# One result block of the last group turned back on VectorE instead of TensorE, and PSUM pairs that alternate across experts

## The chip, the cores and the metric

The kernel runs on one core of a Trainium2 chip. The metric is the device time of one execution in microseconds (us). TensorE (PE, with its weight loads PEld), VectorE (DVE), ScalarE (ACT), GpSimd (POOL) and SyncE (SP) each work through their own instruction queue in program order; they wait for one another through semaphores. Transfers between DRAM and the on-chip memory SBUF are DMAs, most of them issued by SyncE. Matmuls write PSUM, which has eight banks of 128 x 512 fp32.

## The reference

```
# attention, blocks of 64 with a carried state: q, k, v are (4, 8, 768, 64)
out[block] = ((q k^T) * decay mask) v + (q * lam_pow) kv_state
kv_state   = lam_block * kv_state + (k * rev_pow)^T v
# bridge: x is (3072, 512), then four experts, all of them over all tokens
p   = domain_probs / (domain_probs.sum(-1) + 1e-9)
out = sum over e of p[:, e] * (relu(x @ w1[e]) @ w2[e])      # w1 512x1024, w2 1024x512
```

All of it is fp32. The output is 3072 x 512.

## The kernel before

**Groups and units.** The 3072 tokens are three groups of 1024. A *unit* is a group with an expert, so there are twelve, `units[0]` to `units[11]`; `at` is the unit's number. While a unit's second matrix product (h times w2) runs, TensorE also runs the first product (x times w1) of the unit after it (`ahead`), in alternation: the list `order` has eight places, four of the second product `b` and four of the first product `a`. The last unit (`at` 11, group 2, expert 3) has no first product beside it.

**Strassen twice.** Each product is a Strassen-Winograd product of seven block products named M1 to M7, and the first product is split the same way once more: seven outer times seven inner products. In the last group (`nested`) the second product is nested too. `nested_product(e, m, tags)` (from line 1084) gives the steps of one outer product: seven inner products in the order `INNER` = M1, M7, M6, M4, M5, M2, M3, each two fp32 matmuls of 128x256 (the trace has two records for each fp32 matmul). Inner products M1, M6, M5, M3 go to the PSUM bank `tags[0]`, the others to `tags[1]`. M1, M7 and M2 start their bank anew; before M1 does so, whatever was read last from that bank must have been read. After each inner product VectorE adds the bank to a tile `sums[m]` in SBUF (line 1114); for expert 0 some of these are copies on ScalarE (line 1112).

**PSUM pairs.** The outer products of one expert come in the order `SEQ3` = M1, M3, M5, M7, M6, M2, M4 (index `i`). With a unit ahead they take the pairs (q01, q02) and (q11, q12) by `i % 2`, so that products 1 and 7 both have (q01, q02). In the last unit three pairs rotate by `i % 3`, the third being (g1, g3), which the first product uses otherwise.

**The last group is computed turned.** Its second product has features on the partitions and tokens along the rows: `sums[m]` is a tile [128, 4, 256], and `sums[m][:, 2*dd + t]` holds 128 features of block `dd` for 256 tokens of block `t`. After the last expert, the `sums` of M1 to M7 are joined into the four result blocks M2, M3, M4 and M5 (`RESULT`, line 1008). `to_join(m)` fills the list `joins` with steps; each brings one half of a `sums` tile into a PSUM bank with a copy on ScalarE (`bring`, line 968) or adds such a bank to another `sums` tile on VectorE (`add`, line 972). After M6 there are nine steps, and one is taken at each place of the order (`joined()`). In VectorE's queue the product M2's stage then has: M6 into M7 and M3 (three additions), the drain of M2's first bank, M6 into M3's second half, M7 into M4 (two), M7 into M5's first half, the drain of M2's second bank, M7 into M5's second half.

**M2 of the last expert** is a plain product (`plain_product`, line 1032): four parts of eight matmul records, at places 1, 3, 5 and 7 of the order, on banks g1 and g3.

**Turning back.** `give(m, t, tags, dds)` (line 1010) turns a block back: TensorE transposes (128x128, line 1018) into bank s0 or s1, a copy on ScalarE (line 1022) into a tile `y`, and a store by SyncE (line 1024): with both `dds` 256 rows of 1 KB. It first calls `joined(m)`, which takes steps from `joins` until none is left that adds to m. `after_last` says at which places this happens. In the last unit's product M2, M3's two halves are given at places 6 and 7; in its product M4 the halves of M5 and M2 at places 1 to 4. M4's own block is given at the very end: `turn_end`, `turned_product` and two calls of `give` with one `dd`, inserted into `b`.

**Transposes on VectorE in 32x32 blocks** exist already for q and k of some chunks (line 516, `turn_across`), together with copies in DRAM in pieces of 128 bytes (`bring_across`, line 367), issued by SyncE.

Of the kernel before, what the change touches and what calls it, by code (L numbers as in the profile page):

```python
# [22 lines left out]
def kernel(  # L23
# [30 lines left out]
    nc = tc.nc  # L54
# [4 lines left out]
    P = nc.NUM_PARTITIONS  # L59
# [4 lines left out]
    G = CPG * C  # L64
    NG = NTOK // G
    Q = G // 4
    DH = DOUT // 2
    W = 512
# [19 lines left out]
    def bank(tag, name):  # L88
        return ps.tile([P, W], FP32, name=name, tag=tag)

    def small(name):
        return pool.tile([P, W], FP32, name=name, tag="t")
# [329 lines left out]
    for r in range(2):  # L422
        for ac in range(NHP):
            h = 4 * r + ac
            nc.vector.tensor_tensor_scan(
                out=s_decay[:, r, ac], data0=lam_bc[:, h:h + 1].to_broadcast([P, C]), data1=ident[:],
# [9 lines left out]
    m = 1  # L436
    while m < C:
        nc.vector.tensor_tensor(
            out=q_decay[:, :, m:2 * m], in0=q_decay[:, :, 0:m],
# [44 lines left out]
    def take(queue, force=False):  # L484
        for x, f in enumerate(queue):
            if force or getattr(f, "at", 0) <= now[0] and getattr(f, "can", lambda: True)():
                queue.pop(x)()
                return

    def rest(n=1, force=False):  # L490
        for _ in range(n):
            take(background, force)
# [181 lines left out]
    LAST = NG - 1  # L674
# [252 lines left out]
    SEQ3 = ("M1", "M3", "M5", "M7", "M6", "M2", "M4")  # L927
    sums = {}
# [28 lines left out]
    joins, apart, there = [], [], {}  # L957

    def join(a, b):
        def step():  # L960
            x, y = (sums[m][:].rearrange("p k t -> p (k t)") for m in (a, b))
            tt(nc.gpsimd, x, x, y, ALU.add)
            apart.remove(a)

        apart.append(a)
        aside.append(step)
# [8 lines left out]
        x = sums[a][:, 2 * k:2 * k + 2].rearrange("p k t -> p (k t)")  # L975
        tt(nc.vector, x, x, there[b, k][:], ALU.add)

    def joined(m=None):

        while m in apart:  # L980
            take(aside, True)
        while joins and (m is None or any(m in x for x, _ in joins)):
            joins.pop(0)[1]()
            if m is None:
                return

    def to_join(m):

        def steps(*work):
            for fs in work:  # L990
                joins.append(([x[1] for x in fs if x[0] == add], lambda fs=fs: [x[0](*x[1:]) for x in fs]))

        if m == "M3":
            steps(
                [(bring, "M1", 0, "q01")], [(bring, "M1", 1, "q02"), (add, "M6", "M1", 0)], [(add, "M6", "M1", 1)],
            )
        if m == "M5":
            join("M3", "M5")
            join("M2", "M1")
        if m == "M6":  # L1000
            steps(
                [(bring, "M6", 0, "s0")], [(bring, "M6", 1, "s1"), (add, "M7", "M6", 0)], [(add, "M3", "M6", 0)],
                [(bring, "M7", 0, "q11"), (add, "M7", "M6", 1)], [(bring, "M7", 1, "q12"), (add, "M3", "M6", 1)],
                [(add, "M4", "M7", 0)], [(add, "M4", "M7", 1)], [(add, "M5", "M7", 0)], [(add, "M5", "M7", 1)],
            )


    RESULT = {"M2": (0, 0), "M3": (0, 1), "M4": (1, 0), "M5": (1, 1)}

    def give(m, t, tags, dds=(0, 1)):  # L1010

        joined(m)
        i, j = RESULT[m]
        p, o = bank(tags[t % len(tags)], "yp"), small("y")
        w = len(dds) * P
        for x, dd in enumerate(dds):
            for s in range(2):
                nc.tensor.transpose(
                    out=p[:, s * w + x * P:s * w + (x + 1) * P], in_=sums[m][:, 2 * dd + t, s * P:(s + 1) * P],
                    identity=ident[:],  # L1020
                )
        nc.scalar.copy(out=o[:, 0:2 * w], in_=p[:, 0:2 * w])
        r, d = LAST * G + j * W + t * 256, i * DH + dds[0] * P
        nc.sync.dma_start(
            out=out[r:r + 256, d:d + w].rearrange("(s p) d -> p s d", p=P),
            in_=o[:, 0:2 * w].rearrange("p (s d) -> p s d", s=2),
        )


    PLAIN = E - 1, "M2"  # L1030
# [23 lines left out]
    END = E - 1, SEQ3[-1]  # L1054
    ends = []

    def turn_end(t, tag):

        joined(END[1])
        p = bank(tag, "yp")  # L1060
        for s in range(2):
            nc.tensor.matmul(
                out=p[:, s * P:(s + 1) * P], lhsT=sums[END[1]][:, t, s * P:(s + 1) * P], rhs=ident[:],
                is_transpose=True, start=(s == 0), stop=True, skip_group_check=True,
            )
        ends.append(p)
# [300 lines left out]
    def pause_till(i, x):  # L1367
# [13 lines left out]

    fill3 = [(e, m, k) for e in range(E) for m in SEQ3 for k in range(4)]
    after_last = {
        "M2": (None,) * 5 + (("M3", 0), ("M3", 1)),
        "M4": (("M5", 0), ("M5", 1), ("M2", 0), ("M2", 1)),
    }
    steps = attention(1)
    PACE = 1.0, 1.4, 1.0
    for at, (g, e) in enumerate(units):
        if at == 0:  # L1390
            chores.extend(prepare_w2(2) + prepare_w1(3) + prepare_w2(3) + prepare_w1(0))
        ahead = units[at + 1] if at + 1 < len(units) else None
        nested, nests = g == LAST, ahead and ahead[0] == LAST
        if g == LAST - 1:
            if e == 0:
                chores.append(turn_gates)
            chores.extend(prepare_w2_ops(e))
        if ahead and ahead[1] == 0:
            assert not steps
            steps = attention(ahead[0] + 1) if ahead[0] + 1 < NG else []  # L1400
        if at == 3:
            bring_across(3)
        blocks, banks = {}, {}
        for i in range(7):
            if fill2:
                feed2(*fill2.pop(0))
            if nested or (nests and i == 6):
                for _ in range(2 if ahead else 16 if i == 0 else 4 if i > 1 else 0):
                    if fill3:
                        feed3(*fill3.pop(0))  # L1410
            if nests and i == 2:
                nc.scalar.dma_start(
                    out=gate_bc, in_=gate_rows[:, ahead[1]].partition_broadcast(P),
                )
            if nested:
                b = nested_product(e, SEQ3[i], (("q01", "q02"), ("q11", "q12"), ("g1", "g3"))[i % (2 if ahead else 3)])
                if i < 6 and (e, SEQ3[i + 1]) != PLAIN:
                    inner_sums(e, SEQ3[i + 1])
            else:
                b = second_product(g, e, SEQ2[i], banks)  # L1420
            if nests and i == 6:
                inner_sums(ahead[1], SEQ3[0], nested)
                if ahead[1] == EARLY[0]:
                    inner_sums(*EARLY, True)
            a = []
            if ahead:
                a = first_product(*ahead, SEQ[i], blocks, ("g1", "g3"))
            if (e, SEQ3[i]) == END:
                b[6:6] = [lambda: (give("M4", 1, ("s0", "s1"), (1,)), turn_end(1, "q11"))]
                b[5:5] = [lambda: (give("M4", 0, ("s0", "s1"), (1,)), turn_end(0, "q12"))]  # L1430
            if not ahead:
                order = [[], b[0:2], [], b[2:4], [], b[4:6], [], b[6:]]
            elif nested:
                order = [b[0:2], a[0:2], b[2:4], a[2:4], b[4:6], a[4:6], b[6:8], a[6:8]]
            else:
                order = [b[0:1], a[0:2], b[1:2], a[2:4], b[2:3], a[4:6], b[3:5], a[6:8]]
            turned_back = list(after_last.get(SEQ3[i], ())) if nested and not ahead else []
            for x, part in enumerate(order):
                for f in part:
                    if f:  # L1440
                        f()
                now[0] += 1
                if joins:
                    joined()
                elif (ahead or x % 2 == 0 and x + i) and not (nests and i == 6 and x == 7):
                    rest()
                if nested or nests:
                    take(aside)
                if at == 0:
                    take(own_sums)  # L1450
                if nested and ahead and x in (1, 3) and fill3:
                    feed3(*fill3.pop(0))
                if turned_back and x > 0:
                    y = turned_back.pop(0)
                    if y:
                        give(*y[:2], ("s0", "s1"), *y[2:])
                if x == 0 and at * 7 + i >= 6 and fill:
                    feed(*fill.pop(0))
                if at == 0 and x == 0 and i < AHEAD:
                    load(CPG + i)  # L1460
                if steps and (at > 0 or i > 1) and (x == 5 or (x == 2 and i in (1, 3, 5) and at not in (0, 3))):
                    steps.pop(0)()
                if x % 2:
                    trickle()
                pump(PACE[g])
# [30 lines left out]
```

## Time and profile before

| | |
|---|---|
| time of four runs | 1186.0, 1186.87, 1187.85, 1189.48 us; median 1187.36 |
| the profiled execution: its time | 1187.19 us |
| its span, first to last instruction | 1185.4 us |
| granted TensorE clock | 1.00 |
| unit 8 to 9, 9 to 10, 10 to 11 | near 964, 1049 and 1134 us |
| last unit, products M1 to M6 | 1134 to 1165 us |
| last unit, product M2 | 1165 to 1173 us |
| last unit, product M4 and the end | 1173 us to the end |
| last store issued | 1182.54 us |
| DMA traffic | 324 MB, mean 274 GB/s |

The page of a profile gives the busy time of each engine, the span in slices, the chain of work that ended last, and groups of instructions by line and tile. A *timeline* row gives the start in us, the time that the group took, the engine, the line, the operation, output and input tiles, the shape, the count, and in brackets the idle time before it with what ended that idle time. A *waits* row says who waited for whom: total us, times, longest. A row of one line's instructions gives the shortest, median and longest duration in ns. Lines are those of the kernel; line 95 is the helper `tt` through which all tensor-tensor operations pass, so there one goes by the tile's name.

### The profile page before, as it was taken

Reading aid. Unit: us, or ns where it says so; the run is one execution under the profiler, and the core shown is the slowest. Engines: PE = TensorE matmul, PEld = TensorE weight load, DVE = VectorE, ACT = ScalarE, POOL = GpSimd, SP = SyncE. Lnnn points to the kernel's source line nnn. Section 1 sums busy time; section 2 is a strip of 40 time slices with the busy share of each in tenths; the row PEclk is TensorE's granted clock in tenths of the full one; section 3 lists DMA queues with packets and bytes.
Section 4 is the critical chain, followed back from the end, with each engine's and each line's share of the span. In section 5 each row is a group of like instructions: output and inputs, shape, how many; then the busy total and the mean of one; then the engine's idle time right before and its main releaser. Section 6 shows DMA issues by size and latency. Waiting matters only on the chain.

```text
span 1185.4 us, 17886 instructions
## 1 busy us (share of the span) xinstructions
PE 1178.2 (99%) x6567; PEld 1024.3 (86%) x6567; DVE 790.7 (67%) x1329; ACT 275.0 (23%) x502; POOL 628.3 (53%) x600
## 2 busy tenths in 40 slices
PE   9999999999999999999999999999999999999998
PEld 8888888888888888888888888888888888888887
DVE  5785785567478857647756764773665676777784
ACT  3332122112111201211220120121243342341332
POOL 2756258349457800055244655416584683783884
PEclk9999999999999999999999999999999999999999
DMA  9798798999999997899997989898986657566542
GB/s 224 201 279 255 244 304 308 342 339 335 359 366 337 317 297 221 254 284 335 295 298 248 288 291 316 273 307 304 317 294 233 257 189 273 209 239 246 213 160 90
DMA packets 261927, 324.23 MB, mean 274 GB/s; under 512 B 117296, under 2 KB 203216, under 8 KB 261840
## 3 DMA queue, kind: packets, MB, share of 16 engines
q1 hardware_dynamic: 252288, 320.40, 81.3%
q10 hardware_dynamic: 9552, 2.69, 1.2%
q8 instruction: 52, 0.85, 0.3%
q14 instruction: 35, 0.29, 0.1%
HBM read 237.69 MB, written 89.54 MB: 276 GB/s over the span
## 4 chain that ended last, share of the span: by engine, by line
PE 91%; DVE 3%; SPq 2%; DMA 2%; issue 0%; ACT 0%; POOL 0%; ACTq 0%; DVEq 0%
PE pg L843 38%; PE q L897 31%; PE pq L1104 13%; PE pc L1234 2%; PE sp L551 1%; PE op L579 1%; SPq L123 1%; PE pM L1234 1%; DMA w_ops<-ops 1%; DVE hS L95 1%; DVE m L95 1%; DMA w_ops<-w2b 1%; PE op L574 1%; PE op L587 1%; PE pM L1039 1%; SPq L341 0%
## 5 line engine op out<-in xcount | busy, mean ns | idle before, releaser
L843 PE MATMUL pg<-xs_in,ws_in 128*128 128x256 f32 x1960 | 469.8, 380 | 1.1 <-DVE m L95 1.1
L843 PEld LDWEIGHTS pg<-xs_in,ws_in 128*128 128x128 f32 x1960 | 371.3, 190 | 53.1 <-DVE m L95 2.5
L95 DVE TENSOR_TENSOR m<-pg,m 128x512 f32<-128x512 f32 x451 | 307.7, 687 | 106.1 <-PE pg L843 98.8
L897 PE MATMUL q<-w2t,hS 128*128 128x256 f32 x1024 | 243.4, 380 | 0.0
L897 PEld LDWEIGHTS q<-w2t,hS 128*128 128x128 f32 x1024 | 193.2, 190 | 27.0 <-issue 0.2
L913 DVE SCALAR_TENSOR_TENSOR acc<-q,gate,acc 128x256 f32<-128x256 f32 x192 | 92.5, 482 | 169.4 <-PE q L897 169.2
L897 PE MATMUL q<-w2t,m 128*128 128x256 f32 x768 | 182.7, 381 | 0.0
L897 PEld LDWEIGHTS q<-w2t,m 128*128 128x128 f32 x768 | 144.8, 190 | 20.5 <-issue 0.3
L855 ACT ACTIVATE m<-m 128x512 f32<-128x512 f32 x132 | 82.9, 630 | 284.3 <-DVE m L95 283.6
L95 POOL TENSOR_TENSOR m<-m,xT 128x512 f32<-128x512 f32 x64 | 80.6, 1274 | 72.8 <-ACT m L855 55.1
L95 POOL TENSOR_TENSOR kn<-kn,s_decay 128x512 f32<-128x512 f32 x20 | 22.9, 1146 | 142.2 <-PE kp L529 136.4
L95 DVE TENSOR_TENSOR sums<-pq,sums 128x256 f32<-128x256 f32 x153 | 64.3, 421 | 47.4 <-PE pq L1104 40.2
L851 ACT COPY m<-pg 128x512 f32<-128x512 f32 x88 | 51.5, 585 | 174.9 <-PE pg L843 172.1
L1104 PE MATMUL pq<-acc,w2t 128*128 128x256 f32 x352 | 86.6, 379 | 0.0
L95 POOL TENSOR_TENSOR ops<-w2b 128x256 f32<-128x256 f32 x24 | 17.8, 762 | 121.3 <-DMA w2b<-in_moe_w_dram 113.7
L1104 PEld LDWEIGHTS pq<-acc,w2t 128*128 128x128 f32 x352 | 66.8, 190 | 9.3 <-issue 0.3
L95 POOL TENSOR_TENSOR acc<-hT,hT 128x512 f32<-128x512 f32 x32 | 40.2, 1271 | 31.3 <-PE pq L1104 29.4
L95 POOL TENSOR_TENSOR w2o<-w2b 128x512 f32<-128x512 f32 x32 | 40.5, 1288 | 24.8 <-DMA w2b<-in_moe_w_dram 16.4
L786 ACT ACTIVATE m<-m 128x512 f32<-128x512 f32 x44 | 27.7, 631 | 103.1 <-DVE m L95 103.1
L95 DVE TENSOR_TENSOR m<-m,m 128x512 f32<-128x512 f32 x56 | 50.3, 897 | 0.0
L95 DVE TENSOR_TENSOR hS<-m,m 128x512 f32<-128x512 f32 x56 | 46.1, 826 | 4.9 <-ACT m L855 4.9
L95 POOL TENSOR_TENSOR acc<-hT,acc 128x512 f32<-128x512 f32 x32 | 40.7, 1273 | 7.4 <-PE pq L1104 5.4
(157 smaller groups left out, 1360.4 us busy)
## 6 DMA issues: line engine op xcount, KB each, us to landing
xs_in<-x_ops SPq DMA_DIRECT2D x70, 896.0 KB, 6.1
ws_in<-w_ops SPq DMA_DIRECT2D x70, 896.0 KB, 8.7
w2t<-w_ops SPq DMA_DIRECT2D x66, 256.0 KB, 6.6
w2t<-w_sums SPq DMA_DIRECT2D x64, 256.0 KB, 3.9
w_ops<-ops SPq DMA_DIRECT2D x28, 512.0 KB, 5.5
w2t<-in_moe_w_dram SPq DMA_DIRECT2D x48, 256.0 KB, 3.3
w2b<-in_moe_w_dram SPq DMA_DIRECT2D x32, 256.0 KB, 6.1
w_sums<-w2o SPq DMA_DIRECT2D x16, 512.0 KB, 4.9
```

Source lines behind the costliest of these rows:

```text
L95: eng.tensor_tensor(out=o, in0=a, in1=b, op=op)
L123: by.dma_start(out=to[:, :, r], in_=of[:, :, r])
L551: nc.tensor.matmul(out=sp[r][:, ac * C:(ac + 1) * C], lhsT=hc(kT)[half[r], ac], rhs=hc(qT)[half[r], ac], start=True, stop=True,)
L574: nc.tensor.matmul(out=op[r][half[x], a * C:(a + 1) * C], lhsT=kv[half[r], 2 * a + x], rhs=hc(qs)[half[r], 2 * a + x], start=(a == 0), sto ...
L786: nc.scalar.activation(out=o[:], in_=o[:], func=AF.Relu)
L843: nc.tensor.matmul(out=p[:, j * 256:(j + 1) * 256], lhsT=ws[i][:, j * P:(j + 1) * P], rhs=xs[i], start=(fresh and j == 0), stop=True, skip ...
L851: nc.scalar.copy(out=new[at][:], in_=p[:])
L855: nc.scalar.activation(out=new[at][:], in_=new[at][:], func=AF.Relu)
L897: nc.tensor.matmul(out=p[:, s * DH:(s + 1) * DH], lhsT=h[A_OF[m]][:, c * 256 + s * P:c * 256 + (s + 1) * P], rhs=fed2[g, e, m][uu][:, c], ...
L913: nc.vector.scalar_tensor_tensor(out=o, in0=x, scalar=w, in1=o, op0=ALU.mult, op1=ALU.add)
L1104: nc.tensor.matmul(out=p[:, 0:256], lhsT=fed3[e, m, x // 2][:, x % 2, c * P:(c + 1) * P], rhs=b[B_OF[i]][:, c * 256:(c + 1) * 256], start= ...
L1234: nc.tensor.matmul(out=p[:, s * 256:(s + 1) * 256], lhsT=a[c][:, f:f + P], rhs=b[:, c, j * 256:(j + 1) * 256], start=(s == 0 and c == 0 an ...
```

## The change

Three edits.

1. M3's result block no longer goes through `give`. A new function `give_across` lets VectorE transpose each half `sums["M3"][:, 2*dd + t]` (128x256) in 32x32 blocks into a tile `y` and, when both `t` of a `dd` are there, issues four stores, one for each 32 partitions of the tile: 512 pieces of 128 bytes, 64 KB. The second of each four is issued by ScalarE, the others by SyncE. It happens at places 3 (`dd` 0) and 5 (`dd` 1) of product M2, where `give` for M3 stood at 6 and 7.
2. `joined` takes a `k`: with it, only the additions to that half of a block are waited for. `joins` notes pairs (block, half) for that.
3. With a unit ahead, the PSUM pair is chosen by `(at * 7 + i) % 2` instead of `i % 2`. The last unit keeps `i % 3`.

The condition `nested and` before END changes nothing that is emitted: without nesting `b` is shorter than the places where the two calls are inserted, and they are never run.

```diff
-    def joined(m=None):
+    def joined(m=None, k=None):
 
         while m in apart:
             take(aside, True)
-        while joins and (m is None or any(m in x for x, _ in joins)):
+        while joins and (m is None or any(m == x and k in (None, y) for to, _ in joins for x, y in to)):
             joins.pop(0)[1]()
             if m is None:
                 return
...
-                joins.append(([x[1] for x in fs if x[0] == add], lambda fs=fs: [x[0](*x[1:]) for x in fs]))
+                joins.append(([(x[1], x[3]) for x in fs if x[0] == add], lambda fs=fs: [x[0](*x[1:]) for x in fs]))
...
+    halved = {}
+
+    def give_across(m, dd, t):
+
+
+        joined(m, dd)
+        i, j = RESULT[m]
+        if t == 0:
+            halved[m, dd] = small("y")
+        o = halved[m, dd]
+        nc.vector.transpose(out=o[:, t * 256:(t + 1) * 256], in_=sums[m][:, 2 * dd + t])
+        r, d = LAST * G + j * W, i * DH + dd * P
+        for a in range(4 * t):
+            by = nc.scalar if a == 1 else nc.sync
+            by.dma_start(
+                out=out[r:r + W, d + a * 32:d + (a + 1) * 32].rearrange("(b p) d -> p b d", p=32),
+                in_=o[a * 32:(a + 1) * 32].rearrange("p (b d) -> p b d", d=32),
+            )
...
     after_last = {
-        "M2": (None,) * 5 + (("M3", 0), ("M3", 1)),
-        "M4": (("M5", 0), ("M5", 1), ("M2", 0), ("M2", 1)),
+        "M2": ((), (), (("M3", 0, 0), ("M3", 0, 1)), (), (("M3", 1, 0), ("M3", 1, 1))),
+        "M4": ((("M5", 0),), (("M5", 1),), (("M2", 0),), (("M2", 1),)),
     }
...
             if nested:
-                b = nested_product(e, SEQ3[i], (("q01", "q02"), ("q11", "q12"), ("g1", "g3"))[i % (2 if ahead else 3)])
+                pair = (at * 7 + i) % 2 if ahead else i % 3
+                b = nested_product(e, SEQ3[i], (("q01", "q02"), ("q11", "q12"), ("g1", "g3"))[pair])
...
-            if (e, SEQ3[i]) == END:
+            if nested and (e, SEQ3[i]) == END:
...
                 if turned_back and x > 0:
-                    y = turned_back.pop(0)
-                    if y:
-                        give(*y[:2], ("s0", "s1"), *y[2:])
+                    for y in turned_back.pop(0):
+                        if SEQ3[i] == END[1]:
+                            give(*y[:2], ("s0", "s1"), *y[2:])
+                        else:
+                            give_across(*y)
```

## The prediction

> **What bounds the kernel.** I read the page's busy times first, then the waits of TensorE from 950 us on (the change touches nothing earlier), then the timelines around the changes of expert and around the last seventeen microseconds.
>
> ```profile
> PE 1178.2 (99%) x6567; PEld 1024.3 (86%) x6567; DVE 790.7 (67%) x1329; ACT 275.0 (23%) x502; POOL 628.3 (53%) x600
> ```
> ```profile
> PEld pq L1104 <- ACT sums L1112: 0.9, 1, 0.9
> PEld pq L1104 <- ACT m L855: 0.8, 2, 0.4
> ```
>
> TensorE is the clock of this kernel: 7.2 us of the span are not matmul. A microsecond is won only by taking matmuls off TensorE or by closing one of its few gaps. The second fence shows gaps: before the first weights of an expert's first product the weight load waited once 0.9 us, and twice 0.4 us. These are the three changes of expert inside the last group, at 964, 1049 and 1134 us.
>
> **Part 1: alternating PSUM pairs.** Before, product 7 of an expert and product 1 of the next both used q01/q02, so product 1 had to wait until the last block of product 7 had been read out of q01. With (at*7+i)%2 experts 0 to 1 and 1 to 2 change pairs (units 8, 9, 10 begin with pair 0, 1, 0). Unit 10 ends on pair 0 and unit 11 begins on pair 0 (i%3), so the wait at 1134 us stays. It adds no instruction.
>
> ```profile
> 962.82 1.03 PE L843 MATMUL pg<-xs_in,ws_in 128*128 128x256 f32 x4
> 964.35 1.13 PE L1104 MATMUL pq<-m,w2t 128*128 128x256 f32 x4 [0.51 <-ACT sums L1112]
> 965.32 1.03 PE L1104 MATMUL pq<-acc,w2t 128*128 128x256 f32 x4
> 966.18 0.60 PE L843 MATMUL pg<-xs_in,ws_in 128*128 128x256 f32 x2
> ```
>
> Eight of these matmul records take 1.73 us on the chain of waits, 0.216 us each. From 962.82 to 966.18 twelve records stand: 12 x 0.216 = 2.59, but 3.36 passed, so this change of expert costs **0.77 us** (the wait and a slow start of 0.1 to 0.2 us after it). In the same way 1048.20 to 1051.06 is 2.86, a cost of **0.27 us**. There the name ACT m is misleading: the record ahead of the weight load waited until 1049.20, just behind VectorE's read of q01 (1048.74 + 0.41 = 1049.15).
>
> What is late next? After two parts of the second product TensorE returns to the first product and needs bank g1, whose last reader on VectorE is an addition that waits for ScalarE, not for TensorE:
>
> ```profile
> 964.03 0.69 DVE L95 TENSOR_TENSOR hT<-hp,m 128x512 f32<-128x512 f32 x1 [0.59 <-ACT hp L702]
> 964.64 0.68 DVE L95 TENSOR_TENSOR m<-pg,m 128x512 f32<-128x512 f32 x1
> ```
>
> It ends at 965.32. The g1 weight load, at 965.97 before, would come at 965.20 and must wait to about 965.37; the second g1 matmul then starts near 965.69 (0.32 us after such a load, as at 964.35 to 964.67) in place of 966.40. Of 0.77 us 0.71 is left. At 1050 us the same addition ends at 1050.70; its load moves from 1050.84 to 1050.75, the second matmul from 1051.27 to about 1051.07: 0.20 of 0.27 is left. GpSimd's sums are in time (the one for the third part ends at 965.22, needed at 967.1). DMA was busy 0.62 to 0.66 of these stretches, so I cost the earlier loads at nothing; if they were late, the gain would shrink to zero, not below. Sum: **-0.91 us**, between 0 and -1.04.
>
> **Part 2: M3's block turned on VectorE.** It removes from TensorE eight transposes in two lots of four, the x4 rows below, and from ScalarE two copies of 0.585 us and from SyncE two stores.
>
> ```profile
> 1165.43 5.34 PE L1039 MATMUL pM<-m,w2s 128*128 128x256 f32 x24
> 1170.61 0.60 PE L1018 MATMUL yp<-ident,sums 128*128 128x128 f32 x4
> 1171.04 1.89 PE L1039 MATMUL pM<-m,w2s 128*128 128x256 f32 x8
> 1172.77 0.60 PE L1018 MATMUL yp<-ident,sums 128*128 128x128 f32 x4
> 1173.21 1.03 PE L1104 MATMUL pq<-hT,w2s 128*128 128x256 f32 x4
> 1174.08 1.03 PE L1104 MATMUL pq<-acc,w2s 128*128 128x256 f32 x4
> 1174.94 1.04 PE L1018 MATMUL yp<-ident,sums 128*128 128x128 f32 x8
> ```
>
> From 1170.61 to 1171.04 and from 1172.77 to 1173.21 is 0.87 us of TensorE, with no wait. In their place VectorE gets four transposes of 128x256 ahead of work that TensorE needs soon:
>
> ```profile
> L516 DVE STREAM_TRANSPOSE qx<-qx x8: 700/702/703, 335.6 to 650.7; 128x512 f32<-128x512 f32 x8
> ```
> ```profile
> 1169.15 0.69 DVE L95 TENSOR_TENSOR sums<-pM,sums 128x512 f32<-128x512 f32 x1 [0.56 <-PE pM L1039]
> 1169.76 2.47 DVE L95 TENSOR_TENSOR sums<-sums,jp 128x512 f32<-128x512 f32 x4
> 1172.97 0.69 DVE L95 TENSOR_TENSOR sums<-pM,sums 128x512 f32<-128x512 f32 x1 [0.75 <-PE pM L1039]
> 1173.58 0.68 DVE L95 TENSOR_TENSOR sums<-sums,jp 128x512 f32<-128x512 f32 x1
> ```
>
> A 128x512 transpose holds the engine as long as a 128x512 addition (0.62 to the next start against 0.60). 128x256 additions follow one another at 0.34 to 0.35, so I take 0.35 for the half-size transpose; the bounds are 0.31 (half) and 0.62 (no saving). Program order on VectorE becomes: drain, join of M3, two transposes, two joins of M4, two transposes, first join of M5, drain, second join of M5. From 1169.15, which TensorE sets as before: 0.61 + 0.60 + 0.70 + 1.20 + 0.70 + 0.60 + 0.61 + 0.68 = 5.70, so the second join of M5 ends at **1174.85** where it ended at 1174.26.
>
> That join is what M5's turning-back waits for. TensorE, 0.87 us earlier, would load the first weights that depend on it at 1174.18 (1175.05 before). It waits to about 1174.89: 0.71 of the 0.87 us is handed back, and a slow restart takes up to 0.1 more. Left is **-0.1 us**. With 0.31 for a transpose 0.3 is left; with 0.62 the wait is 1.8 us and the change loses 0.9. Behind the waiting transposes stand M4's reads of q01/q02; they come at 1174.8 to 1175.5, before TensorE needs the banks again at 1175.6 and later. ScalarE's two fine stores wait for the transposes until 1171.1 and 1173.0, and its next copy is due only at 1175.4.
>
> One page of the Trainium skill leans the other way, in favour of the edit: "VectorE: DVE Perf Modes", section "The three transpose paths", prices a 128x128 bf16 transpose at 390 ns on TensorE and 311 ns on VectorE. By that as an estimate eight times 390 ns, 3.1 us, would leave TensorE. The rows say 0.11 us for each transpose on TensorE, so the gain cannot reach that.
>
> **The fine stores.** Eight stores of 512 pieces of 128 bytes take the place of two with 256 pieces of 1 KB. The nearest row is the copy of q and k between DRAM buffers, of the same 512 pieces of 128 bytes:
>
> ```profile
> L367 SPq DMA_DIRECT2D across<-in_q_dram x32: 562/680/3231, 66.7 to 446.2; - x32
> ```
>
> Issue takes 0.56 to 3.23 us, median 0.68; the long ones stood in full queues (DMA shares near 1), while here no packet moves between 1168 and 1172 us. Six on SyncE at 0.62 each run from 1171.2 to 1175.0; M5's first store is due at 1176.0, so there is 1 us of slack. A packet of 128 bytes took 13 ns against 46 ns for 1 KB: 4096 x 13 / 16 engines = 3.3 us of DMA against 512 x 46 / 16 = 1.5 us, over by about 1179, with the last store issued at 1182.5. Cost: nothing; if the cover is gone, see the third rival. "DMA: Bandwidth & Descriptors", section "Specifications", speaks against the edit: below 512 bytes a transfer does a read-modify-write. It gives no time for it; per byte the packet rows already show 128 bytes at 2.2 times the cost of 1 KB.
>
> **Sum.** -0.91 - 0.1 = -1.0 us. The profiled execution took 1187.19 us (span 1185.4 and 1.8 around it), the median of the four runs is 1187.36. So 1186.2 for the profiled execution, **1186.4 us** for the median. Not over 0.2% (2.4 us), which is about what a measurement of this kernel can tell from no change; the runs before alone span 1186.0 to 1189.5.
>
> **Rivals.**
> - *Everything is kept* (15%): VectorE keeps up, and all 0.77 + 0.27 + 0.87 = 1.9 us stay: 1185.5. For it: VectorE was idle 0.56 and 0.75 us in this stage. Against: the new transposes need 1.4.
> - *The changes of expert win nothing* (15%): another wait stands right behind (the g1 bank, or the loads) and part 2 also gives back its gain: 1187.3. For it: the g1 bank is within 0.2 us of being that wait at both places.
> - *Slower: SyncE's issue of fine stores delays the last store* (9%). If each of the six takes p, M5's store starts at 1171.2 + 6p and the last one seven stores of 0.49 later. That passes the old 1182.4 once p is over 1.3 us. At 1.93, as one such issue at 403 us took in a busy stretch, the last store starts at 1186.2, 3.8 us late: about 1190.2 with part 1's gain. Against it: idle queues.
> - *The alternation does not do all it says*: unit 10 to 11 keeps its wait. This is already in the sum.
>
> The forecast has the remaining 61%, its own range 1185.7 to 1187.0. Run-to-run spread moves a median by about 0.8 us; with the first rival's 1185.5 and the second's 1187.3 the range is 1184.6 to 1188.4, which leaves out the third and little else. Faster by over 0.2% (below 1185.0) needs the first rival and a lucky median: 13%. Slower by over 0.2% (above 1189.7) is the third rival, with a little for longer transposes plus an unlucky median: 11%. Within: 76%.
>
> **What would show it.** Part 1: no wait on ACT sums before the weight load near 964, none near 1049, still one near 1133; g1's weight load waits for VectorE instead. Part 2: no x4 rows of L1018, four STREAM_TRANSPOSE rows of about 0.43 us between 1169 and 1173, and one new wait of about 0.7 us of M5's transposes for VectorE. Fine stores: issue near 0.6 us, none unfinished when the last store is issued. The prediction is wrong if that issue is over 1.3 us, or if TensorE meets M5 without a wait.

## The result, and the profile after

The changed kernel takes 1186.32 us in the median of 34 runs (1184.63 to 1187.72), the kernel before 1187.82 us in 52 runs (1185.88 to 1191.18). The ratio is 0.9988 with a 95% interval of 0.9983 to 0.9993: about 1.4 us less (0.8 to 2.0 by the interval), clear of no change, but inside the 0.2% that the prediction gave as about the least that can be told from it. The profiled execution has a span of 1184.4 us (1185.4 before).

So small a difference is read from stretches of the trace, not from whole times. The start of the last group's second product moves from run to run by more than the change is worth: its first matmul record stands at 879.08 us before, at 879.48 after, and between 879.05 and 881.20 in the experiments. From that record on, two executions of the changed kernel agree to 0.01 us, record by record; so do the kernels here that use the same PSUM pairs, up to product M2. I call the stretch from it to the last matmul record the *nested part*; it lasts 302.75 us before and 301.54 after.

The waits of the weight loads from 950 us on, after:

```profile
PEld pg L1123 <- DVE sums L95: 0.7, 1, 0.7
PEld yp L1018 <- DVE sums L95: 0.6, 1, 0.6
PEld pg L843 <- DVE m L95: 0.4, 2, 0.2
PEld pq L1123 <- ACT m L855: 0.4, 1, 0.4
```

(Line 1123 is line 1104 of before, 1058 is 1039.) The 0.9 us for ACT sums is gone, one of the two 0.4 us for ACT m is left, and three waits stand where the prediction put them: two of 0.2 us for bank g1 at the changes of expert, one of 0.6 us at the transposes. The 0.7 us of the first row were there before too.

The first change of expert on TensorE, and the weight loads and VectorE's queue at the second:

```profile
963.23 1.03 PE L843 MATMUL pg<-xs_in,ws_in 128*128 128x256 f32 x4
964.09 1.03 PE L1123 MATMUL pq<-m,w2t 128*128 128x256 f32 x4
964.95 1.03 PE L1123 MATMUL pq<-acc,w2t 128*128 128x256 f32 x4
```
```profile
1049.41 0.84 PEld L1123 LDWEIGHTS pq<-acc,w2t 128*128 128x128 f32 x4
1050.45 1.59 PEld L843 LDWEIGHTS pg<-xs_in,ws_in 128*128 128x128 f32 x8 [0.20 <-DVE m L95]
```
```profile
1049.11 0.69 DVE L95 TENSOR_TENSOR hT<-hp,m 128x512 f32<-128x512 f32 x1 [0.25 <-ACT hp L702]
1049.72 0.68 DVE L95 TENSOR_TENSOR m<-pg,m 128x512 f32<-128x512 f32 x1
```

Product 1's matmuls follow without a gap. Two parts later the load for g1 starts at 1050.45, 0.05 us after the addition that reads g1 ends (1049.72 + 0.68). A gap was closed and a shorter one opened behind it.

The stage of product M2 and the start of M4, TensorE and VectorE:

```profile
1172.70 1.03 PE L1123 MATMUL pq<-acc,w2s 128*128 128x256 f32 x4
1173.56 0.38 PE L1018 MATMUL yp<-ident,sums 128*128 128x128 f32 x2
1174.29 0.87 PE L1018 MATMUL yp<-ident,sums 128*128 128x128 f32 x6 [0.35 <-DVE sums L95]
1175.00 1.89 PE L1123 MATMUL pq<-acc,w2s 128*128 128x256 f32 x8
```
```profile
1168.65 0.69 DVE L95 TENSOR_TENSOR sums<-pM,sums 128x512 f32<-128x512 f32 x1 [0.56 <-PE pM L1058]
1169.26 0.68 DVE L95 TENSOR_TENSOR sums<-sums,jp 128x512 f32<-128x512 f32 x1
1169.86 0.76 DVE L1039 STREAM_TRANSPOSE y<-sums 128x256 f32<-128x256 f32 x2
1170.55 1.24 DVE L95 TENSOR_TENSOR sums<-sums,jp 128x512 f32<-128x512 f32 x2
1171.72 0.75 DVE L1039 STREAM_TRANSPOSE y<-sums 128x256 f32<-128x256 f32 x2
1172.39 0.65 DVE L95 TENSOR_TENSOR sums<-sums,jp 128x512 f32<-128x512 f32 x1
1172.97 0.68 DVE L95 TENSOR_TENSOR sums<-pM,sums 128x512 f32<-128x512 f32 x1
1173.57 0.67 DVE L95 TENSOR_TENSOR sums<-sums,jp 128x512 f32<-128x512 f32 x1
```

The eight transposes of M5 (2 + 6) took 0.87 us before; now 1.44 us pass from 1173.56 to 1175.00. TensorE does the two that need only M5's first half, then waits until VectorE's last row above is done (1174.24). VectorE no longer waits for the second drain, as it did before for 0.75 us: it comes late to it.

### The profile page after: what moved, and what is told of

It is laid out like the page before. It is cut to its first block, busy times and chain, and to the rows that moved or that the text cites. A ratio compares the mean times of both kernels' runs of the same rounds, so it can differ in the third digit from the quotient of the medians.

```text
span 1184.4 us, 17880 instructions
## 1 busy us (share of the span) xinstructions
PE 1176.6 (99%) x6559; PEld 1023.0 (86%) x6559; DVE 791.4 (67%) x1333; ACT 274.0 (23%) x500; POOL 629.0 (53%) x600
## 4 chain that ended last, share of the span: by engine, by line
PE 91%; DVE 3%; DMA 3%; SPq 1%; POOL 1%; issue 0%; ACT 0%; ACTq 0%; DVEq 0%; POOLq 0%
PE pg L843 37%; PE q L897 30%; PE pq L1123 13%; PE pM L1253 2%; PE pc L1253 2%; PE op L579 2%; PE sp L551 2%; DMA w_ops<-ops 2%; DMA w_ops<-w2o 1%; PE op L574 1%; DVE hS L95 1%; SPq L123 1%; DVE m L95 1%; PE op L587 1%; DVE sums L95 0%; PE kp L529 0%
```

## The experiments

Theory: TensorE sets the time; the alternation wins 0.71 and 0.20 us, the turning wins its 0.87 us less what VectorE's longer queue makes TensorE wait at M5, and the fine stores cost nothing where they stand. Rivals: the gain lies in stretches that the change does not touch; it lies mostly in the turning; the wait at M5 is for something else; the fine stores cost time.

| kernel | nested part, us | last matmul to the end, us | ratio to before, 95% interval |
|---|---|---|---|
| before | 302.75 | 3.58 | 1 |
| changed | 301.54 | 3.41 | 0.9988 (0.9983 to 0.9993) |
| changed again (e0) | 301.54 | 3.42 | 0.9988 (0.9979 to 0.9997) |
| pairs alone (e1) | 301.85 | 3.59 | 0.9995 (0.9986 to 1.0004) |
| turning alone (e2) | 302.44 | 3.41 | 0.9995 (0.9987 to 1.0004) |
| last unit on the other pair (e3) | 301.84 | 3.42 | one run |
| two transposes twice (e5) | 302.50 | 3.42 | one run |
| coarse stores (e6) | 301.54 | 3.51 | one run |
| second half late (e4) | 300.97 | 3.42 | 0.9982 (0.9973 to 0.9991) |
| all turned late (e7) | 300.98 | 6.59 | one run |

**The changed kernel again.** No edit.

> The changed kernel unaltered, to see what repeats. Theory (gains where predicted): the stretch from the first product's last part before unit 9 to the same place before unit 10 is again 84.7 us and not 85.4; TensorE waits 0.5 to 0.6 us at M5's transposes; the stretch up to 950 us may come out up to 0.5 us longer or shorter than before without meaning. Time 0.9985 to 0.9993 of before. Rival (the gain lies in the stretches that the change does not touch): the stretch up to 950 us is shorter than before in proportion to the gain.

The nested part is the same to 0.01 us, and the stretch between the first two changes of expert is again 84.67 us (85.38 before). The stretch up to the nested part was 0.12 us shorter than in the first profile, and 0.29 us longer than before: in these profiles it has no part in the gain. That rival falls.

**The pairs alone.**

```diff
-  (("q01", "q02"), ("q11", "q12"), ("g1", "g3"))[i % (2 if ahead else 3)]
+  (("q01", "q02"), ("q11", "q12"), ("g1", "g3"))[(at * 7 + i) % 2 if ahead else i % 3]
```

> Only the alternating pairs; M3 is turned back on TensorE as before. Theory: -0.71 us at 964 and -0.20 us at 1049 stay, everything from 1165 us on takes as long as before; -0.9 us in all, 0.9992 of before. Rival (most of the gain is M3's turning on VectorE): -0.3 us or less, 0.9997 or more.

302.75 - 301.85 = 0.90 us, all of it at the two changes of expert: from the record behind the second change to the last one, the distance to the kernel before stays the same to 0.01 us. The interval of the whole times does not tell it from no change.

**The turning alone.**

```diff
-                pair = (at * 7 + i) % 2 if ahead else i % 3
+                pair = i % (2 if ahead else 3)
```

> Only M3's turning on VectorE; the pairs by i % 2 as before. Theory: the waits of 0.77 and 0.27 us at the changes of expert are back; from 1165 us to the end -0.3 us, TensorE waits 0.5 us for VectorE at M5's transposes; -0.3 us in all, 0.9997 of before. Rival (most of the gain is M3's turning): -0.9 us, 0.9992.

```profile
PEld pq L1123 <- ACT sums L1131: 0.9, 1, 0.9
PEld pq L1123 <- ACT m L855: 0.8, 2, 0.4
PEld pg L1123 <- DVE sums L95: 0.7, 1, 0.7
PEld yp L1018 <- DVE sums L95: 0.6, 1, 0.6
```

The waits of before are back in the first two rows, the new wait at M5 is there in the fourth. The nested part is 302.75 - 302.44 = 0.31 us shorter. The two edits add up: 0.90 + 0.31 = 1.21, the whole kernel's gain there. Here too the interval of the whole times does not tell the gain from no change.

**The two transposes of the second half, twice.**

```diff
-        nc.vector.transpose(out=o[:, t * 256:(t + 1) * 256], in_=sums[m][:, 2 * dd + t])
+        for _ in range(1 + dd):
+            nc.vector.transpose(out=o[:, t * 256:(t + 1) * 256], in_=sums[m][:, 2 * dd + t])
```

> The changed kernel with the two transposes of M3's second half issued twice, into the same tile. Theory (VectorE's queue sets the wait at M5): two more at 0.34 us, all of it on the path: TensorE waits 1.2 us in place of 0.5 to 0.6 there, and the nested part lasts 302.2 us in place of 301.54. Rival (VectorE has slack there): no more than 301.6 us.

```profile
1171.87 1.72 DVE L1040 STREAM_TRANSPOSE y<-sums 128x256 f32<-128x256 f32 x4
1173.51 0.65 DVE L95 TENSOR_TENSOR sums<-sums,jp 128x512 f32<-128x512 f32 x1
```

The nested part is 0.96 us longer than in the changed kernel, not 0.66. My price for two more transposes was too low here: the four hold VectorE for 1.64 us (1171.87 to 1173.51) where the two held it for 0.67 (1171.72 to 1172.39), 0.97 more. A transpose that is written over the output of the one before starts 0.46 and 0.44 us behind it here; in the run with everything turned late, where each of four has an output of its own, they follow one another at 0.36, 0.33 and 0.33 us. What VectorE loses, TensorE loses: 0.97 against 0.96. So VectorE's queue has no slack at this place.

**The second half turned late.** M3's second half goes behind M5's in product M4.

```diff
-        "M2": ((), (), (("M3", 0, 0), ("M3", 0, 1)), (), (("M3", 1, 0), ("M3", 1, 1))),
-        "M4": ((("M5", 0),), (("M5", 1),), (("M2", 0),), (("M2", 1),)),
+        "M2": ((), (), (("M3", 0, 0), ("M3", 0, 1)), ()),
+        "M4": ((("M5", 0),), (("M5", 1), ("M3", 1, 0), ("M3", 1, 1)), (("M2", 0),), (("M2", 1),)),
...
-                        if SEQ3[i] == END[1]:
+                        if y[0] != "M3":
```

> The changed kernel, with M3's second half (two transposes, four fine stores) moved behind the turning back of M5's second half, at place 2 of product M4, so that no transpose stands ahead of M5's second join in VectorE's queue. Theory (VectorE's queue makes TensorE wait at M5): M5's second join ends near 1173.7 us and the wait is gone; another 0.5 to 0.57 us less than the changed kernel, 0.9980 to 0.9985 of before if the rest repeats. Rival 1 (TensorE waits there for something else, a bank or a copy): the wait stays near 0.5 us. Rival 2 (fine stores are expensive when late): the last store starts later than its copy allows and the time is as the changed kernel's or longer.

```profile
1172.94 1.03 PE L1123 MATMUL pq<-acc,w2s 128*128 128x256 f32 x4
1173.80 1.04 PE L1018 MATMUL yp<-ident,sums 128*128 128x128 f32 x8
1174.67 1.89 PE L1123 MATMUL pq<-acc,w2s 128*128 128x256 f32 x8
```

The eight transposes of M5 run in one piece and take 0.87 us again. The nested part is 0.57 us shorter than in the changed kernel, the whole of what was handed back: the wait was for VectorE's queue, and rival 1 falls. So does rival 2: the last store is issued 0.71 us after the last matmul record, as in the changed kernel. This version is the fastest of all, 0.9982 of before (0.9973 to 0.9991); its interval overlaps that of the changed kernel, so only the nested part shows that it beats that one.

**Coarse stores.** The same tiles, stored by four plain DMAs.

```diff
-        for a in range(4 * t):
...
+        if t == 1:
+            for x in range(2):
+                nc.sync.dma_start(
+                    out=out[r + 256 * x:r + 256 * x + 256, d:d + P].rearrange("(s p) d -> p s d", p=P),
+                    in_=o[:, x * 256:(x + 1) * 256].rearrange("p (s d) -> p s d", s=2),
+                )
```

> The changed kernel with M3's eight fine stores replaced by four plain ones of 256 pieces of 512 bytes from the same tiles. It leaves out the order within M3's block of the output (the 32x32 blocks land where they lie in the tile). Theory (the fine stores are covered): nothing moves, 301.54 us for the nested part and 3.4 us from its last matmul to the end, within 0.1 and 0.2. Rival (they cost something in queues or DMA): either gets shorter by more than that.

Nothing moves: 301.54 us, and the end is within 0.1 us (0.10 longer, not shorter). Where the change puts them, the fine stores are covered.

**Everything turned late.** All four transposes and eight fine stores at place 4 of product M4.

```diff
-        "M2": ((), (), (("M3", 0, 0), ("M3", 0, 1)), (), (("M3", 1, 0), ("M3", 1, 1))),
-        "M4": ((("M5", 0),), (("M5", 1),), (("M2", 0),), (("M2", 1),)),
+        "M2": (),
+        "M4": ((("M5", 0),), (("M5", 1),), (("M2", 0),), (("M2", 1), ("M3", 0, 0), ("M3", 0, 1), ("M3", 1, 0), ("M3", 1, 1))),
```

> The changed kernel with all four transposes and eight fine stores moved behind M2's turning back, at place 4 of product M4, just ahead of the last four stores. Theory (what counts is TensorE's path until the last store waits for SyncE): the wait at M5 is gone as with the second half alone, so the nested part lasts 301.0 us; six fine stores of about 0.48 us on SyncE begin near 1178 us, end near 1181, and the last store starts 0 to 0.5 us later after its last matmul than before (0.71 us); the end 0 to 0.5 us later for that. Rival (the third of the prediction: fine stores so near the end cost microseconds): the last store starts over 1 us later, and the whole is slower than the changed kernel.

SyncE's issues in this kernel:

```profile
1174.49 3.49 SPq L1024 DMA_DIRECT2D out_dram<-y  x4
1178.08 4.12 SPq L1043 DMA_DIRECT2D out_dram<-y  x6
1182.30 0.46 SPq L1024 DMA_DIRECT2D out_dram<-y  x1
1182.86 0.42 SPq L1098 DMA_DIRECT2D out_dram<-y  x1
1183.37 0.45 SPq L1024 DMA_DIRECT2D out_dram<-y  x1
1183.91 0.45 SPq L1098 DMA_DIRECT2D out_dram<-y  x1
```

Half of my expectation fails, and the rival holds. TensorE's part is as short as expected, but the last store starts 3.77 us after the last matmul record and not 0.71: I had counted the six fine stores and forgotten that the four stores of M4 queue behind them. Six take 4.12 us and not 2.9, since one of them took 1.40; M4's four take another 2.06 to the end of the last issue. From the nested part's first matmul to the end it is 307.57 us, against 306.33 before and 304.95 changed. The cost that the prediction's third rival spoke of, fine stores that hold up the last store in SyncE's queue, is real; the place of the stores is what spares the change.

**The last unit on the other pair.**

```diff
-                pair = (at * 7 + i) % 2 if ahead else i % 3
+                pair = (at * 7 + i) % 2 if ahead else (1, 0, 2, 1, 0, 2, 0)[i]
```

> The changed kernel, with the last unit beginning on (q11, q12) as well (its seven products take the pairs 1, 0, 2, 1, 0, 2, 0 of the three), so that the last change of expert changes pairs too. Theory (a wait closed is worth only what the next one behind it leaves): the 0.20 us late start near 1133 us is gone, but there is no first product between the parts here, so the third part meets VectorE's read of the first bank at once, and that read stands in a queue that TensorE does not set; 0 to 0.1 us less from the nested part's first matmul to its last (301.54 us before this edit). Rival (each pair change is worth its own wait): 0.27 us less, 301.27.

```profile
1133.01 1.03 PE L1123 MATMUL pq<-m,w2t 128*128 128x256 f32 x4
1133.87 1.03 PE L1123 MATMUL pq<-acc,w2t 128*128 128x256 f32 x4
1135.08 2.83 PE L1123 MATMUL pq<-acc,w2t 128*128 128x256 f32 x12 [0.18 <-issue]
...
1146.54 1.03 PE L1123 MATMUL pg<-acc,w2s 128*128 128x256 f32 x4
1148.14 2.90 PE L1123 MATMUL pg<-acc,w2s 128*128 128x256 f32 x12 [0.58 <-DVE sums L95]
```

ScalarE's copies for the join of M1, in the changed kernel:

```profile
1141.75 1.10 ACT L970 COPY jp<-sums 128x512 f32<-128x512 f32 x2
```

And here, with VectorE's queue behind them:

```profile
1146.35 1.11 ACT L970 COPY jp<-sums 128x512 f32<-128x512 f32 x2 [4.97 <-DVE sums L95]
1146.98 0.69 DVE L95 TENSOR_TENSOR sums<-sums,jp 128x512 f32<-128x512 f32 x1 [0.66 <-ACT jp L970]
1147.58 0.75 DVE L95 TENSOR_TENSOR sums<-pg,sums 128x256 f32<-128x256 f32 x2
```

The last change of expert is closed: from the first product's last part to product 1 it is 0.86 us, 1.06 in the changed kernel. The third part then starts late (1135.08, where 1133.87 + 0.86 = 1134.73 would do), and four parts of product 1 on, TensorE is where it was: from that last part of the first product to the row x8 behind these, 5.59 us pass in both kernels. So far the theory holds, with a gain of 0.00. But the rotation also changes what happens in product M5, where TensorE now loses 0.74 us before its third part (1146.54 + 0.86 = 1147.40 to 1148.14), and the nested part comes out 0.30 us longer than the changed kernel's: 0.44 of the 0.74 come back at TensorE's next wait for VectorE, 0.66 us in the changed kernel and 0.20 here. That I had not expected. The code and the rows say where it comes from. The join of M1 copies into q01 and q02. In the changed kernel product M3 runs on q11 and q12, and the copies start early; here M3 runs on q01 and q02, and the copies start only when VectorE has read M3's last part (1145.90 + 0.41 = 1146.31). The addition that needs them stands in VectorE's queue ahead of the read of M5's first bank, and for that read, done at 1148.00, the third part waits. No run gave the copies other banks to confirm it.

## Why the prediction was right

**Which bound.** TensorE's path sets the time of the last group: every experiment moved the end by what it moved TensorE, to within 0.2 us (the last section has that rest), except the one in which SyncE's queue took over.

**Part 1** was right in mechanism and size. The matmuls of two products (112 records), counted from the last part ahead of the change of expert, took 24.95 us and now take 24.24 (0.71 less); at the second change 24.44 became 24.24 (0.20 less), as the sum said; and the wait near 1133 us stayed. It came out because the sum did not stop at the removed wait: the next reader in VectorE's queue, which did not move with TensorE, was followed.

**Part 2** was right in mechanism; the term mis-sized is the hand-back at M5. The prediction had 0.71 us and up to 0.1 for a slow restart, so 0.1 us left; the runs show 0.57 handed back and 0.31 left. VectorE's queue took 5.59 us from its start at 1168.65 to the end of M5's second join, not 5.70: pairs of transposes took 0.69 and 0.67, not 0.70, and an addition behind a transpose frees VectorE after about 0.58, not 0.60. And TensorE lost only 0.06 us in the restart: its weight load is normally 0.1 us ahead of its matmul, so a load late by 0.62 made a matmul late by 0.51.

**The fine stores** cost nothing, as predicted, with more room than predicted. SyncE's issues took 0.32 to 0.52 us, not 0.62:

```profile
L1043 SPq DMA_DIRECT2D out_dram<-y x6: 315/484/520, 1170.6 to 1173.4; - x6
DMA to landing us min/median/max: 1.9/2.1/2.2
```

They land in 1.9 to 2.2 us. The coarse stores of the experiment, with twice the bytes in each, do so in 1.8 to 1.9:

```profile
DMA to landing us min/median/max: 1.8/1.8/1.9
```

The Trainium skill, "DMA: Bandwidth & Descriptors", section "Specifications", has transfers below 512 bytes do a read-modify-write. The fine stores do land up to 0.3 us later with half the bytes; whether a read-modify-write is the reason no run here shows, and nothing waits for it.

**The sum** came out at 1.4 us where 1.0 was forecast: 0.91 + 0.31 + 0.17. The last term, between the last matmul and the end, was not in it at all (see the last section). That the forecast of 1186.4 us lies so near the measured 1186.32 is luck in part: the median before was 1187.36 in four runs and is 1187.82 in 52, and this error nearly cancels the 0.4 us by which the sum was short.

## What to carry to other kernels

When a wait is closed on the engine that sets the time, find the next semaphore that engine waits for and ask whether its releaser moves along; here that gave each gain to 0.01 us. Work moved to an idle engine is free only if it does not stand ahead of something the bounding engine needs soon: the two transposes of M3's second half cost 0.57 us ahead of a join and nothing behind it. And count a queue to its end: stores that are free in the middle cost 3 us when the last ones queue behind them.

## What was not expected of the hardware

Over the last 300 us two executions of the changed kernel agree to 0.01 us, and over the 285 us up to product M2 so do the kernels here that use the same PSUM pairs, although their first 880 us differ by up to 2 us.

From the last store's issue to the end it takes 2.87 us before and 2.70 changed. SyncE's final checks of the stores' semaphores follow one another at 0.06 us; the semaphore of the last store is in the first of five checks before (four are left when it lands), in the second with coarse stores, in the third in the changed kernel, since the number of stores shifts which one it gets. From the end of the check that waited for the last store to the end of the execution it takes 1.05, 0.98 and 0.92 us: 0.06 us less for each check that is no longer left. That is 0.13 of the 0.17 us. The other 0.04 are in the last store itself, which lands 1.80 us after its issue before and 1.76 us in the changed kernel. This part of the gain comes with the number of stores and not with TensorE's path, and it was not tried by itself.
